# Half of the groups of three bias tables: the multiply by x goes from VectorE to ScalarE and GpSimd

## The chip, the core and the metric

The kernel runs on one core of a Trainium2 chip. The core has five engines that work side by side, each on its own queue of instructions in order: TensorE (PE in the profile) multiplies matrices into PSUM, VectorE (DVE) and ScalarE (ACT) compute element by element and reach both PSUM and SBUF, GpSimd (POOL) works on SBUF, and SyncE (SP) issues most of the transfers between the chip's main memory and SBUF. The metric is the device time of the whole program in microseconds; less is better. The time before is 1106.28 us, the median of three runs.

## What is computed

Attention over 4 batches, 8 heads, 576 positions and head size 64 with a bias that a small network makes from the positions, then two expert blocks, cut here to what matters:

```python
scores = (1 / sqrt(64)) * q @ k.T
rel = pos[:, None] - pos[None, :]
x = log1p(abs(rel)) / log1p(maximum(pos[:, None], 1))      # 576 x 576
h = maximum(x[..., None] * w1 + b1, 0)                     # 32 hidden units
bias = h @ w2                                              # one value per head
attn = softmax(scores + bias) @ v
y = moe1(attn)     # w_in, h * softmax(h), layer norm, w_out
out = moe2(y)      # sigmoid gate, value, w_out2
```

For one entry of the table, each hidden unit is either off or linear in x. So the bias of a head is a slope times x plus an offset, where slope and offset are sums over the units that are on at this x.

## The kernel before

**Bias tables.** The 576 rows of positions are made as five tables: tables 0 to 3 have 128 rows each, table 4 the last 64. `bias_tile(t)` makes table t group by group: `bias_mask` (lines 344 to 368) lets VectorE compare distances with thresholds, which gives a 0/1 mask of the units that are on (float16, 2048 elements in each partition), and `bias_grp` (lines 383 to 436) does the rest two groups later. Tables 0 to 3 have nine groups, table 4 has five.

**A group.** TensorE multiplies the masks with the weights into a PSUM bank (`bp`, line 409). For every pair of positions this gives 32 columns with the slope part (8 heads, 4 rows) and 32 with the offset part. For the later tables a group is done in two parts of 8 steps, each with a bank of its own from a pool of three (`ps_m`) that is shared with the transposes of q, k and of the attention's result. Then come two steps: the slope part times x into the tile `btmp` (a pool of two), and the sum with the offset part into the table (line 434, always VectorE). The first step has two forms, and the counter `nbg`, which goes up by one with every group over all tables, chooses:

```python
if nbg[0] % BD < (BD0 if t < 2 else BD1):          # 427
    dve.tensor_tensor(out=hg(tmp, 0), in0=hg(ps, 0), in1=xb_, op=ALU.mult)
else:
    act.activation(out=tmp, in_=ps[:, :, 0:32], func=ACTF.Copy)          # 430
    pool.tensor_tensor(out=hg(tmp, 0), in0=hg(tmp, 0), in1=xb_, op=ALU.mult)   # 431
```

BD is 4. For the first two tables BD0 = 0, so all groups take the second form: ScalarE copies the slope part out of PSUM (GpSimd does not read PSUM) and GpSimd multiplies. For tables 2, 3 and 4 BD1 = 4, so all groups take the first form.

**Where it stands in the program.** Tables 0 and 1 are made at the start and used from SBUF. Tables 4, 2, 3, in this order, are side work: `side_work` (line 955) hands out steps in turn, first alternating with the steps that decode and split the first expert's weights (`w1_steps`: ScalarE line 168, VectorE lines 169 to 173, GpSimd lines 177 and 639), then alone; five steps go with each tick of attention. A finished part of a table is stored to main memory by SyncE (lines 438 to 448) and loaded again when attention needs it. A tick is two heads of one block of rows: scores on TensorE (line 500), scores plus bias with the row maximum on VectorE (line 520), a factor (line 525) and the exponential on ScalarE (line 527), the float16 high part on ScalarE or VectorE (lines 538 and 536), the low part on GpSimd (lines 539 and 540), a transpose by DMA that SyncE issues (line 542), and the product with v on TensorE (line 560). There are 72 ticks. When tables and weights are ready, the first expert's steps take the place of the side work (lines 691 to 770); the second expert follows (lines 1025 to 1352).

**Order.** The program is written in this sequence, with a priority for attention's instructions; for most of it the order of each engine's queue is then laid out ahead of time with a simulated timeline, so a change of one instruction can shift the order of others. Once an engine runs, it takes its queue in order.

Of the kernel before, what the change touches and what calls it, by code (L numbers as in the profile page):

```python
# [51 lines left out]
TAILQ = 1  # L52
BD = 4
BD0 = 0
BD1 = 4
NFR = 12
SUMPRIO = 130
W2PRIO = 300
# [30 lines left out]
def attn_moe_kernel(  # L89
# [293 lines left out]
    def bias_grp(t, grp, bs):  # L383
# [18 lines left out]
        for big, a, n in parts:  # L402
# [21 lines left out]
            def hg(ap, o):  # L424
                return ap[:, :, o:o + 32].rearrange("p j (h g) -> p j h g", g=4)

            if nbg[0] % BD < (BD0 if t < 2 else BD1):
                dve.tensor_tensor(out=hg(tmp, 0), in0=hg(ps, 0), in1=xb_, op=ALU.mult)
# [992 lines left out]
```

## Time and profile before

| | us |
|---|---|
| median of three runs | 1106.28 |
| lowest, highest | 1100.22, 1108.24 |
| the profiled execution | 1103.77 |
| its span, first to last instruction | 1102.0 |

A profile shows one execution. Busy time is the time in which an engine ran an instruction; a wait is the idle time ahead of an instruction, put down to what released it. PE's granted clock is a share of full speed. Lines such as L428 are lines of the kernel; names left of the arrow are the tile that is written, right of it those that are read.

| whole span | busy us | share |
|---|---|---|
| TensorE matmuls | 911.8 | 83% |
| VectorE | 811.1 | 74% |
| ScalarE | 627.5 | 57% |
| GpSimd | 426.4 | 39% |

### The profile page before, as it was taken

The numbers are of one execution on the slowest core, as the hardware profiler recorded it, in microseconds if no ns is written. First come the engines' busy times: TensorE is split into PE (matmuls) and PEld (weight loads), VectorE is DVE, ScalarE is ACT, GpSimd is POOL, SyncE is SP. The second block draws the span as 40 slices with busy tenths as digits, with TensorE's granted clock in tenths as the row PEclk, the third lists the DMA queues.
The fourth block names the chain that finished last, engine by engine and source line by source line (L and its number), as shares of the span: only waits on it lengthen the run. The fifth ranks groups of instructions, "written<-read, shape, count | busy, mean of one in ns | idle before, by whom it ended". The sixth has DMA issues, their size and how long they took to land.

```text
span 1102.0 us, 24792 instructions
## 1 busy us (share of the span) xinstructions
PE 911.8 (83%) x9950; PEld 641.8 (58%) x9950; DVE 811.1 (74%) x1647; ACT 627.5 (57%) x1302; POOL 426.4 (39%) x365
## 2 busy tenths in 40 slices
PE   2554774678778889889999778798999899999998
PEld 2442553456456666767776456343477488488585
DVE  6797999897557776666774889989949568257453
ACT  4858567766567788877883667654323233123232
POOL 2566366473455466545552266749000000000000
PEclk9655666657898999999999899998999999999999
DMA  9948899698979899999957536621000100100000
GB/s 281 306 136 294 179 201 216 132 185 187 211 144 191 183 194 196 185 198 202 211 110 173 163 106 188 188 75 38 20 21 2 66 10 1 48 11 1 20 21 20
DMA packets 259715, 146.41 MB, mean 133 GB/s; under 512 B 216976, under 2 KB 229648, under 8 KB 259600
## 3 DMA queue, kind: packets, MB, share of 16 engines
q1 hardware_dynamic: 258064, 143.25, 55.1%
q0 software_dynamic: 1536, 1.58, 0.5%
q8 instruction: 78, 1.28, 0.5%
q14 instruction: 37, 0.30, 0.1%
HBM read 82.27 MB, written 20.05 MB: 93 GB/s over the span
## 4 chain that ended last, share of the span: by engine, by line
PE 29%; DVE 13%; issue 3%; ACT 2%; DMA 2%; POOL 1%; SPq 0%; POOLq 0%; DVEq 0%; ACTq 0%
PE prod L1229 14%; PE ops L1297 10%; DVE fr L1153 2%; DVE w2f L170 2%; DVE fs L1153 2%; DVE w2f L173 2%; PE x2ps L761 2%; DMA wraw<-in_moe_w_val_dram 1%; DVE gv L1135 1%; PE hps L702 1%; DMA wraw<-in_moe_w_gate_dram 1%; DVE w2f L169 1%; DVE w2s L1153 1%; PE xps L560 1%; DVE fr L1273 1%
## 5 line engine op out<-in xcount | busy, mean ns | idle before, releaser
L539 POOL TENSOR_TENSOR p<-p,p 128x1024 f16<-128x1024 f32 x72 | 154.5, 2146 | 154.3 <-ACT p L538 105.3
L1153 DVE TENSOR_TENSOR fr<-prod,fr 128x512 f32<-128x512 f32 (+1 forms) x154 | 91.8, 614 | 108.1 <-PE prod L1229 104.1
L1297 PE MATMUL ops<-w2f,gv 128*128 128x512 f16 x648 | 144.4, 382 | 4.3 <-DVE gv L1135 3.1
L527 ACT ACTIVATE p<-p,m,sc 128x576 f32<-128x576 f32 x144 | 124.0, 862 | 2.8
L761 PE MATMUL x2ps<-lt,w1f 128*128 128x128 f16 x1728 | 106.5, 221 | 12.7 <-DVE lt L750 11.9
L761 PEld LDWEIGHTS <-w1f 128*128 128x128 f16 x1728 | 100.7, 99 | 22.6 <-issue 18.8
L520 DVE CUSTOM_DVE_ANT_0 p<-s_ps,gk 128x576 f32<-128x576 f32 x144 | 104.2, 751 | 11.7 <-PE s_ps L500 8.6
L1297 PEld LDWEIGHTS <-gv 128*128 128x128 f16 x648 | 63.4, 98 | 79.6 <-DVE gv L1135 3.6
L1267 PE MATMUL s_ps<-xb,w2f 128*128 128x512 f16 x384 | 90.3, 392 | 18.0 <-DVE fr L1273 13.2
L409 PEld LDWEIGHTS <-mask 128*128 128x128 f16 (+1 forms) x1312 | 64.9, 122 | 65.8 <-issue 28.7
L500 PE MATMUL s_ps<-gk,qt 64*128 64x288 f16 (+1 forms) x960 | 94.8, 323 | 9.4 <-DVE m L520 5.4
L1229 PEld LDWEIGHTS <-w2f 128*128 128x128 f16 x1056 | 92.2, 98 | 11.7 <-issue 1.4
L560 PE MATMUL xps<-gk,pt 128*128 128x64 f16 (+1 forms) x2240 | 87.8, 202 | 12.1 <-DMA pt<-p 12.1
L560 PEld LDWEIGHTS <-pt 128*128 128x128 f16 (+1 forms) x2240 | 81.7, 107 | 25.2 <-DMA pt<-p 13.9
L702 PE MATMUL hps<-w1f,xt 128*128 128x512 f16 x312 | 77.9, 401 | 0.6 <-DVE qt L279 0.6
L409 PE MATMUL bp<-rhs,mask 128*128 128x64 f16 (+1 forms) x960 | 53.8, 227 | 29.2 <-DVE gb L434 14.8
L1267 PEld LDWEIGHTS <-w2f 128*128 128x128 f16 x384 | 38.2, 100 | 66.9 <-issue 26.0
L1134 ACT ACTIVATE gv<-fr 128x512 f16<-128x512 f32 (+1 forms) x60 | 34.7, 586 | 70.9 <-DVE fr L1287 65.7
L1229 PEld LDWEIGHTS <-w2s 128*128 128x128 f16 x792 | 69.2, 98 | 7.4 <-issue 0.3
L538 ACT ACTIVATE p<-p 128x1152 f16<-128x1152 f32 x54 | 62.6, 1159 | 14.1 <-DMA pt<-p 12.4
L525 ACT ACTIVATE m<-m,sc 128x1 f32<-128x1 f32 x144 | 40.5, 286 | 48.1 <-DVE m L520 48.0
L702 PEld LDWEIGHTS <-xt 128*128 128x128 f16 x384 | 37.2, 102 | 50.4 <-issue 16.4
(196 smaller groups left out, 1852.9 us busy)
## 6 DMA issues: line engine op xcount, KB each, us to landing
gk<-bias_d SPq DMA_DIRECT2D x24, 576.0 KB, 4.8
wraw<-in_moe_w_out_dram SPq DMA_DIRECT2D x20, 512.0 KB, 4.3
wraw<-in_moe_w_gate_dram SPq DMA_DIRECT2D x12, 512.0 KB, 4.1
wraw<-in_moe_w_val_dram SPq DMA_DIRECT2D x12, 512.0 KB, 3.8
sraw<-in_q_dram SPq DMA_DIRECT2D x12, 384.0 KB, 5.5
sraw<-in_k_dram SPq DMA_DIRECT2D x12, 384.0 KB, 3.8
sraw<-in_v_dram SPq DMA_DIRECT2D x12, 384.0 KB, 4.2
bias_d<-gk SPq DMA_DIRECT2D x8, 576.0 KB, 8.8
```

The lines of the kernel that those rows point to most:

```text
L409: pe.matmul(big[0:np_, jj // 8, o:o + 64], lhsT, rhs[i].rearrange("p c h g -> p (c h g)"), start=(i == 0), stop=(i == 1),)
L500: pe.matmul(ss[hh][p0:p1, n, 0:288], qt[rows, nr * ql + r, p0:p1], kt[rows, o:o + 288], start=(m == 0), stop=(m == 2))
L520: dve.tensor_tensor_reduce(out=pp[:, hh].rearrange("p (i j) -> p i j", i=2), in0=ss[hh][:, :, 0:288], in1=bi.rearrange("p (i j) -> p i j", ...
L527: act.activation(out=pp[:, hh], in_=pp[:, hh], func=ACTF.Exp, bias=m[:, 2 + hh:3 + hh], scale=col(C), accum_out=sm[:, c + hh:c + hh + 1])
L539: pool.tensor_tensor(out=p16[:, :, 640:1152], in0=pp[:, :, 0:512], in1=hi[:, :, 0:512], op=ALU.subtract)
L560: pe.matmul(o, a, b_, start=(n == 0), stop=(n == len(seq) - 1))
L702: pe.matmul(h, xt[:, xl, kk, off:off + 128], win16[:, 2 * kk + n, wl], start=(kk == 0 and xl == 0 and wl == 0), stop=(kk == 3 and xl == 1),)
L761: pe.matmul(ps[:, dc], wout16[:, f, wl, 128 * dc:128 * dc + 128], lt[:, ll, f], start=(n == 0), stop=(n == 23))
L1153: dve.tensor_tensor(out=out_, in0=a, in1=b, op=op)
L1229: pe.matmul(p[:, jf, 0:nn], w(wl, kk, jf), x(xl, kk), start=(m == 0), stop=(m == 5))
L1267: pe.matmul(ps[:, 0:n], w[:, 4 * (j // 4) + c, wl, o:o + 128], xx[:, 0:n, c, xl, :], start=(m == 0), stop=(m == 11))
L1297: pe.matmul(ps, gvs[j // 4][:, gl, j % 4, 128 * tt:128 * tt + 128], w2h16[2][:, j, wl], start=(m == 0), stop=(m == 35))
```

## The change

One constant:

```diff
-BD1 = 4
+BD1 = 2
```

For tables 4, 2 and 3 the test of line 427 now holds for groups with `nbg % 4` of 0 or 1 only. Groups with 2 or 3 take the second form: ScalarE's copy (line 430) and GpSimd's multiply (line 431) in place of VectorE's multiply (line 428). The sum of line 434 stays on VectorE and now takes GpSimd's result. Nothing else in the source differs; tables 0 and 1 are made as before.

## Rows read from the trace of the kernel before

**Rows 1.** Busy time of each engine by stage, whole core (columns in the first line)

```profile
core 0: us, PE busy (x) PEld busy (x) DVE busy (x) ACT busy (x) POOL busy (x), PEclk, DMA share, GB/s
110.00:270.00 160.00, 110.78 (x1517) 83.53 (x1518) 146.93 (x270) 101.80 (x213) 85.64 (x70) 0.63 0.88 183
270.00:600.00 330.00, 291.11 (x4248) 215.69 (x4249) 216.08 (x572) 246.49 (x546) 179.05 (x156) 0.96 0.92 181
...
800.00:1102.00 302.00, 292.75 (x2385) 212.16 (x2382) 174.16 (x313) 85.78 (x147) 0.00 (x0) 0.99 0.06 20
```

**Rows 2.** Waits, 110 to 270 us: us in total, times, longest

```profile
DVE btmp L428 <- PE bp L409: 3.2, 4, 1.4
...
DVE p L520 <- PE s_ps L500: 2.7, 3, 2.1
...
PE bp L409 <- DVE gb L434: 14.8, 9, 6.9
...
POOL p L539 <- ACT p L538: 18.5, 5, 6.0
...
SPq L542 <- POOL w1f L639: 24.1, 7, 6.0
```

**Rows 3.** Lines by form, 110 to 270 us: busy us, mean ns | idle before, releaser

```profile
L539 POOL TENSOR_TENSOR p<-p,p 128x1024 f16<-128x1024 f32 x17 | 36.5, 2145 | 30.8 <-ACT p L538 18.5 <-DVE sums L591 5.0 <-ACT sums L590 3.5
...
L358 DVE TENSOR_TENSOR mask<-dtab_sb,thr 128x2048 f16<-128x2048 f16 x18 | 27.5, 1527 | 0.0
...
L428 DVE TENSOR_TENSOR btmp<-bp,xs 128x256 f32<-128x256 f32 x44 | 24.4, 566 | 3.4 <-PE bp L409 3.2
...
L170 DVE SCALAR_TENSOR_TENSOR w1f<-wraw,w1f 128x512 int32<-128x512 int32 x10 | 10.9, 1093 | 0.0
...
L173 DVE SCALAR_TENSOR_TENSOR w1f<-wraw,w1f 128x512 int32<-128x512 int32 x6 | 6.7, 1120 | 0.1
...
L428 DVE TENSOR_TENSOR btmp<-bp,xs 64x256 f32<-64x256 f32 x2 | 0.8, 404 | 0.0
```

**Rows 4.** Timeline, VectorE and GpSimd near 172, VectorE near 234: start us, us

```profile
172.27 4.53 DVE L358 TENSOR_TENSOR mask<-dtab_sb,thr 128x2048 f16<-128x2048 f16 x1
...
172.08 2.14 POOL L539 TENSOR_TENSOR p<-p,p 128x1024 f16<-128x1024 f32 x1
...
174.55 1.15 POOL L639 TENSOR_TENSOR w1f<-wtmp,w1f 128x512 f16<-128x512 f32 x1
...
233.65 1.10 DVE L428 TENSOR_TENSOR btmp<-bp,xs 128x256 f32<-128x256 f32 x2
234.67 1.22 DVE L358 TENSOR_TENSOR mask<-dtab_sb,thr 128x2048 f16<-128x2048 f16 x1
```

**Rows 5.** Lines by form, 0 to 110 us, tables 0 and 1 (columns as Rows 3)

```profile
L430 ACT ACTIVATE btmp<-bp 128x256 f32<-128x256 f32 x14 | 5.2, 377 | 4.1 <-DVE gk L434 3.9 <-DVE acc L142 0.2
...
L431 POOL TENSOR_TENSOR btmp<-btmp,xs 128x256 f32<-128x256 f32 x14 | 16.1, 1153 | 9.7 <-ACT btmp L430 9.6
```

**Rows 6.** Instructions of single lines: count, ns min/median/max, first and last start us

```profile
L358 DVE TENSOR_TENSOR mask<-dtab_sb,thr x18: 1202/1222/4527, 126.5 to 250.9; 128x2048 f16<-128x2048 f16 x18
...
L170 DVE SCALAR_TENSOR_TENSOR w1f<-wraw,w1f x12: 671/683/2495, 95.3 to 199.6; 128x512 int32<-128x512 int32 x12
...
L173 DVE SCALAR_TENSOR_TENSOR w1f<-wraw,w1f x8: 679/800/2333, 96.6 to 200.4; 128x512 int32<-128x512 int32 x8
...
L428 DVE TENSOR_TENSOR btmp<-bp,xs x46: 403/580/599, 110.8 to 261.2; 128x256 f32<-128x256 f32 x44, 64x256 f32<-64x256 f32 x2
...
L431 POOL TENSOR_TENSOR btmp<-btmp,xs x25: 632/1524/2566, 21.9 to 82.6; 128x256 f32<-128x256 f32 x14, 128x512 f32<-128x512 f32 x11
...
L736 DVE TENSOR_SCALAR mm<-mm x18: 141/154/155, 295.8 to 663.3; 128x1 f32<-128x1 f32 x18
```

**Rows 7.** VectorE's waits over the whole span: us in total, times, longest

```profile
DVE mm L736 <- POOL mm L735: 11.0, 10, 1.8
...
DVE gk L434 <- POOL btmp L431: 5.1, 6, 2.0
```

## Prediction

> **What bounds the kernel now.** I read first the busy times by stage [rows 1]. The three later bias tables are built between 110 and 270 us. In that stage VectorE is busy 146.9 of 160 us (92%), TensorE 110.8, ScalarE 101.8, GpSimd 85.6, and the DMA engines stand at 0.88. After 270 us the picture turns: TensorE is busy 291 of 330 us and the DMA share is 0.92, and from 800 us on it is TensorE alone (293 of 302 us). So the change falls into the one stretch in which VectorE is the busiest engine, and what that stretch gains should move everything behind it as a block: attention blocks, expert blocks and the TensorE tail come in the order of the program, none of them starts by the clock.
>
> Second, the waits in that stage [rows 2]. VectorE's largest sum is 3.2 us (bias products that are late), and for attention's scores it waits 2.7; it lacks work only for moments, so an instruction less is time less, until another engine ends last. TensorE, in contrast, waits 14.8 us for the add of line 434 to give a PSUM bank back. GpSimd waits 18.5 us in five waits for ScalarE's cast of line 538, and the transposes of SyncE's queue wait 24.1 us for GpSimd's weight remainders (line 639). These three bear on the rivals.
>
> **The change part by part.** The group counter nbg stands at 18 when table 4 begins and runs 19 to 41 over the 5+9+9 groups of tables 4, 2 and 3. With BD1 = 4 all 23 groups, two parts each, take line 428: 46 multiplies, 44 of the large form and 2 of the small [rows 3]. With BD1 = 2 a group stays if nbg modulo 4 is 0 or 1. Those that leave are 19, 22, 23, 26, 27, 30, 31, 34, 35, 38 and 39: 11 groups, 22 parts, of which 2 (group 23) have 64 partitions.
>
> *Removed.* VectorE's instructions overlap a little, so I take the distance from start to start and not the duration: two multiplies start at 233.65 and the next instruction at 234.67, 0.51 us each [rows 4], where the group's mean is 0.566 [rows 3]. The small form has 0.404, scaled likewise 0.35. 20 x 0.51 + 2 x 0.35 = 10.9 us leave VectorE.
>
> *Added on ScalarE.* 22 copies from PSUM at 0.377 us [rows 5] are 8.3 us. ScalarE has 58 us idle in the stage, so I cost them at nothing. The cover has one hole: btmp has two buffers, so a copy can stand in ScalarE's queue until an add two parts back is done, with the exponentials of attention behind it. The next operand late would then be line 538's cast, and the transpose behind it. With full cost it is 8.3 us, which I count to the third rival.
>
> *Added on GpSimd.* 22 multiplies of the form that took 1.153 us on average in the first two tables [rows 5], 25.4 us; the shortest took 0.632 [rows 6], which would make 13.9. I take the mean, as VectorE will be as full as it was there. GpSimd goes from 85.6 to some 111 of 160 us. That is not full, but it isn't free: VectorE is held up while GpSimd runs. The row for it is the mask of line 358, 1.2 us at its shortest [rows 6] and 4.53 us at 172.27, while GpSimd ran line 539 from 172.08 and line 639 up to 175.70, with line 540 between [rows 4]. By groups, mean less shortest [rows 3, 6]: line 358 18 x 0.325 = 5.9 us, line 170 10 x 0.42 = 4.2, line 173 6 x 0.44 = 2.6; 12.7 us lost against 85.6 us of GpSimd, 0.148 us each. The 25.4 us added bring 25.4 x 0.148 = 3.8 us of new loss (with 13.9: 2.1). What is taken off VectorE does not suffer itself: line 428's longest is 0.599 [rows 6]. So lock-free work is traded for work that holds up others.
>
> [...]
>
> *Added wait.* The add of line 434 now waits for GpSimd instead of for VectorE's own multiply. Behind it in VectorE's queue stand masks, weight decoding and line 520 of attention, and ScalarE waits for that one. In the first two tables, all made this way, VectorE waited 5.1 us for 25 parts [rows 7], 0.204 each; 22 x 0.204 = 4.5 us. From below it is nothing. From above I take the other place where VectorE takes a result back from GpSimd, line 736: 11.0 us [rows 7] over 18 instructions [rows 6], 0.61 each, 13.4 us. I take 4.5, since it is the same operation, though GpSimd had less else to do there.
>
> *Unchanged.* Matmuls, masks, DMA issues and stores are the same in number. The last two groups (40, 41) stay on VectorE, so the hand-over of the last table gets no longer chain.
>
> *Sum.* -10.9 + 3.8 + 4.5 = -2.6 us. Against the profiled execution's own 1103.77 that is 1101.2; it lies 2.5 us below the median of the three runs, 1106.28, which would give 1103.7. I forecast 1103, nearer to the median because that is what is measured. Ends of this case: -10.9 + 2.1 + 0 = -8.8 (1097 from the median) and -10.9 + 3.8 + 13.4 = +6.3 (1112).
>
> **The rivals.**
>
> 1. *The relief goes through whole.* Neither stalls nor waits: 1106.3 - 10.9 = 1095. For it: VectorE's 92% and its small waits [rows 1, 2]. Against it: the mask's 4.53 us [rows 4], and that the chain now crosses three engines.
>
> 2. *Another bound takes over at once.* The DMA share is 0.88 in the stage and 0.92 after it [rows 1]; if the transposes set the pace, VectorE's free time turns into waits and nothing moves: about 1105. Against it: no wait of VectorE's for a DMA in the stage comes near the top, and SyncE's transposes wait for GpSimd rather than for the wire [rows 2].
>
> 3. *Slower: the multiply stands behind attention in GpSimd's queue.* GpSimd works in order. Five of the 17 large subtractions of line 539 in the stage [rows 3] waited 3.7 us each for ScalarE's cast [rows 2]. If the same share of the 22 multiplies, some 7, stands behind such a one, the add stands still on VectorE for that long, and everything behind it: 7 x 3.7 = 25.9. Then -10.9 + 3.8 + 25.9 = +18.8, about 1124 (1122.6 by the own time, 1125.1 by the median). It decides from a mean wait of (10.9 - 3.8)/22 = 0.32 us per part on; at 0.83 us the kernel is 1% slower. For it: first tables' GpSimd had no attention to serve, so 0.204 is measured under the easier condition; ScalarE's copies of this form waited there 3.9 us for adds, too [rows 5], and TensorE's 14.8 us for PSUM banks [rows 2] can only grow. Against it: the order of each queue is laid out with a simulated timeline, which puts the add where its operand is expected.
>
> 4. *Slower: each multiply stops VectorE for its full length*, as the mask of 4.53 us was stopped. 25.4 takes the place of 3.8: -10.9 + 25.4 + 4.5 = +19.0, about 1124 as well. Against it: 85.6 us of GpSimd now cost 12.7, not 85.6; most of VectorE's instructions read PSUM and run through.
>
> **How the numbers follow.** My forecast has 0.42, rival 1 0.16, rival 2 0.12, rival 3 0.24, rival 4 0.06. A difference of about 1% (11 us) is what a measurement of this kernel tells from no change. Even the whole relief of 10.9 us falls just short of that, so faster by over 1% holds only about half of rival 1 and a little of what a new order of the queues may bring: 0.13. Slower by over 1% is nearly all of rivals 3 and 4: 0.27. The rest, 0.60, lies within. The likeliest case's own range is 1097 to 1112; 8 in 10 takes in rival 1 below and reaches to rivals 3 and 4 above: 1094 to 1124.
>
> **What would show it.** Right: line 428 counts 24 and line 431 47; VectorE's busy time in the stage falls by 5 to 8 us; its wait for line 431 grows by about 4.5 us over the 22 parts, and masks keep a mean near 1.5 to 1.7 us. Wrong towards rival 1: that wait is near nothing and the last multiply of line 428, now at 261.2 [rows 6], comes some 11 us earlier. Towards rival 2: that multiply comes earlier, but the transposes or line 520 then wait, and the distance to the end grows. Towards rival 3: VectorE waits over 7 us for line 431 and the last multiply comes after 262. Towards rival 4: lines 358, 170 and 173 lose over 20 us to GpSimd. What I can't price is the new order that the whole program gets, since each queue is laid out anew; if the stage behaves as said and the end does not follow, that is the reason.

## The result, and the profile after

The changed kernel takes 1118.28 us (median of three runs, 1114.09 to 1120.82) where the kernel before took 1106.28. These two medians stand as 1.0108 to 1; the ratio recorded for the pair is 1.0127, 95% interval 1.0091 to 1.0162, and five later sets of 13 to 22 runs of the kernel before, with medians of 1102.82 to 1105.51, bear out the larger one. It is slower by 1.3%. The forecast was 1103 and no change that can be told; the time lies inside the range given, on the other side of no change.

The profiled execution of after took 1120.82 us with a span of 1119.0; that of before had a span of 1102.0. The profiles are thus 17.0 us apart and the medians 12.0, since the one profiled execution lies above its median and the other below. Three moments split the 17.0 us. The view of single lines gives them (count, ns min/median/max, start of the first and of the last instruction); here line 434 (the sum into the tables) and line 560 (the product with v) of the kernel before:

```profile
core 0 of [0], span 1102.0 us
...
L434 DVE TENSOR_TENSOR gb<-bp,btmp x46: 543/592/628, 111.4 to 261.8; 128x256 f32<-128x256 f32 x44, 64x256 f32<-64x256 f32 x2
...
L560 PE MATMUL xps<-gk,pt x2240: 192/193/262, 115.3 to 598.4; 128*128 128x64 f16 x150, 128*64 128x64 f16 x37
```

and of the changed kernel:

```profile
core 0 of [0], span 1119.0 us
...
L434 DVE TENSOR_TENSOR gb<-bp,btmp x46: 574/593/632, 117.1 to 272.4; 128x256 f32<-128x256 f32 x44, 64x256 f32<-64x256 f32 x2
...
L560 PE MATMUL xps<-gk,pt x2240: 192/193/261, 116.7 to 610.2; 128*128 128x64 f16 x150, 128*64 128x64 f16 x37
```

(In the fences "..." stands for lines left out; where no window is named, a line is from the whole span.) The last sum of the bias tables comes 10.6 us later (261.8 to 272.4), the last product of attention 11.8 us later (598.4 to 610.2), the end 17.0. So the stage of the change loses 10.6, attention behind it hands that on (+1.2), and the tail, from the last product to the end of the span, grows by another 5.2 (503.6 to 508.8), in a stretch where the change moved nothing. These three numbers, **last sum, last product, tail**, are given for every run below. How far they repeat is seen in two runs with the same order of work up to the end of attention, e9 for before and e10 for after: 261.0 and 596.8, 273.4 and 609.5. They hold to 1.6 us in these two. That is no bound, for single runs of the kernel before lie anywhere from 1099.0 to 1111.1 us, while the tails of kernels with one order behind attention agree within 2 us: most of the spread from run to run seems to lie ahead of the last product, and each profile below is one execution. Where it matters, the median is given beside it.

Busy times by stage, as [rows 1]:

```profile
core 0: us, PE busy (x) PEld busy (x) DVE busy (x) ACT busy (x) POOL busy (x), PEclk, DMA share, GB/s
...
110.00:270.00 160.00, 99.26 (x1347) 76.03 (x1347) 129.91 (x232) 103.49 (x230) 106.55 (x92) 0.61 0.86 178
270.00:600.00 330.00, 292.58 (x4229) 219.03 (x4230) 216.76 (x578) 248.27 (x550) 176.13 (x154) 0.94 0.91 181
```

VectorE is relieved (146.9 to 129.9) and GpSimd loaded (85.6 to 106.6), and both TensorE and VectorE do *less* in the same 160 us: the stage isn't short of engine time any more, it waits. The waits from 110 to 270 us, to set beside [rows 2] (us in total, times, longest):

```profile
PE bp L409 <- DVE gb L434: 21.1, 12, 3.9
POOL p L539 <- ACT p L538: 21.1, 7, 7.3
PE xps L560 <- DMA pt<-p: 20.8, 9, 4.6
...
ACT p L538 <- DMA pt<-p: 16.3, 7, 5.3
...
DVE gb L434 <- POOL btmp L431: 10.9, 7, 6.6
...
DVE xn L593 <- PE xps L560: 5.7, 1, 5.7
```

VectorE's longest kind of wait was 3.2 us in sum before; now it waits 10.9 us for the moved multiply, 6.6 of it in one place, and 5.7 for a product with v. The one long event, in the timeline (start, duration, engine, line; in brackets the idle time ahead and its releaser):

```profile
237.35 0.61 PE L560 MATMUL xps<-gk,pt 128*128 128x64 f16 x8 [4.03 <-DMA pt<-p]
237.39 1.16 ACT L538 ACTIVATE p<-p 128x1152 f16<-128x1152 f32 x1 [5.30 <-DMA pt<-p]
...
238.68 2.12 POOL L539 TENSOR_TENSOR p<-p,p 128x1024 f16<-128x1024 f32 x1 [7.35 <-ACT p L538]
238.98 0.64 ACT L430 ACTIVATE btmp<-bp 128x256 f32<-128x256 f32 x2
...
240.76 0.43 POOL L540 TENSOR_TENSOR p<-p,p 128x128 f16<-128x128 f32 x1
241.15 1.15 POOL L639 TENSOR_TENSOR w1f<-wtmp,w1f 128x512 f16<-128x512 f32 x1
242.26 1.66 POOL L431 TENSOR_TENSOR btmp<-btmp,xs 128x256 f32<-128x256 f32 x2
...
243.15 0.61 DVE L434 TENSOR_TENSOR gb<-bp,btmp 128x256 f32<-128x256 f32 x1 [6.62 <-POOL btmp L431]
...
243.81 0.42 PE L409 MATMUL bp<-rhs,mask 128*128 128x64 f16 x5 [3.93 <-DVE gb L434]
```

Read it from the top. A transpose lands late; the product on TensorE and the cast of line 538 on ScalarE wait for it. The copies of line 430 stand behind that cast, GpSimd's subtraction of line 539 waits 7.35 us for it, and the multiplies of line 431 stand behind the subtraction and a weight remainder. VectorE stands 6.62 us at the sum, and TensorE waits for the PSUM bank. Before, no such chain reached VectorE: its multiply read PSUM itself.

### The profile page after: what moved, and what is told of

It reads as the page before. It is cut to its first block, busy times and chain, and to the rows that moved or that the text cites. A ratio compares the mean times of both kernels' runs of the same rounds, so it can differ in the third digit from the quotient of the medians.

```text
span 1119.0 us, 24810 instructions
## 1 busy us (share of the span) xinstructions
PE 917.9 (82%) x9950; PEld 650.0 (58%) x9950; DVE 801.9 (72%) x1625; ACT 631.4 (56%) x1324; POOL 446.5 (40%) x387
## 4 chain that ended last, share of the span: by engine, by line
PE 31%; DVE 12%; DMA 3%; issue 2%; ACT 2%; POOL 1%; SPq 0%; ACTq 0%; POOLq 0%
PE prod L1229 13%; PE ops L1297 11%; DVE fs L1153 2%; DVE fr L1153 2%; PE x2ps L761 2%; PE s_ps L1267 2%; DVE w2f L170 2%; DMA wraw<-in_moe_w_val_dram 2%; DVE w2f L173 1%; DVE gv L1135 1%; PE hps L702 1%; DVE w2s L1153 1%; DMA wraw<-in_moe_w_gate_dram 1%; PE xps L560 1%; DVE w2f L169 1%
## 5 line engine op out<-in xcount | busy, mean ns | idle before, releaser
L761 PE MATMUL x2ps<-lt,w1f 128*128 128x128 f16 x1728 | 111.6, 226 | 13.8 <-DVE lt L750 10.9
L761 PEld LDWEIGHTS <-w1f 128*128 128x128 f16 x1728 | 105.1, 101 | 26.9 <-issue 19.6
L520 DVE CUSTOM_DVE_ANT_0 p<-s_ps,gk 128x576 f32<-128x576 f32 x144 | 104.1, 752 | 20.2 <-PE s_ps L500 16.6
L560 PE MATMUL xps<-gk,pt 128*128 128x64 f16 (+1 forms) x2240 | 91.2, 206 | 20.8 <-DMA pt<-p 20.8
L1267 PE MATMUL s_ps<-xb,w2f 128*128 128x512 f16 x384 | 92.1, 399 | 18.1 <-DVE fr L1273 14.2
L560 PEld LDWEIGHTS <-pt 128*128 128x128 f16 (+1 forms) x2240 | 85.6, 109 | 32.9 <-DMA pt<-p 23.6
L500 PE MATMUL s_ps<-gk,qt 64*128 64x288 f16 (+1 forms) x960 | 90.5, 320 | 10.1 <-DVE m L520 3.9
L702 PE MATMUL hps<-w1f,xt 128*128 128x512 f16 x312 | 75.6, 392 | 0.6 <-DVE qt L279 0.6
L431 POOL TENSOR_TENSOR btmp<-btmp,xs 128x256 f32<-128x256 f32 (+2 forms) x47 | 57.7, 1241 | 40.6 <-ACT btmp L430 39.8
```

What stands on the lines that cost most here:

```text
L500: pe.matmul(ss[hh][p0:p1, n, 0:288], qt[rows, nr * ql + r, p0:p1], kt[rows, o:o + 288], start=(m == 0), stop=(m == 2))
L520: dve.tensor_tensor_reduce(out=pp[:, hh].rearrange("p (i j) -> p i j", i=2), in0=ss[hh][:, :, 0:288], in1=bi.rearrange("p (i j) -> p i j", ...
L560: pe.matmul(o, a, b_, start=(n == 0), stop=(n == len(seq) - 1))
L702: pe.matmul(h, xt[:, xl, kk, off:off + 128], win16[:, 2 * kk + n, wl], start=(kk == 0 and xl == 0 and wl == 0), stop=(kk == 3 and xl == 1),)
L761: pe.matmul(ps[:, dc], wout16[:, f, wl, 128 * dc:128 * dc + 128], lt[:, ll, f], start=(n == 0), stop=(n == 23))
L1267: pe.matmul(ps[:, 0:n], w[:, 4 * (j // 4) + c, wl, o:o + 128], xx[:, 0:n, c, xl, :], start=(m == 0), stop=(m == 11))
```

## The experiments

"Order" below is the order of the instructions in each engine's queue. Each kernel's queues are laid out anew, so every edit moves it. Ratios are to the kernel before, run beside each experiment, with 95% intervals in brackets. Code is cut; "..." stands for what is left out.

### What the relief is worth, and what the load costs

**e1_relief.** The moved multiplies are left out altogether: the sums of the eleven groups take a tile of zeros.

```diff
+skip = t > 1 and nbg[0] % BD >= BD1
-tmp = bp_["tmp"].tile(...)[0:np_]
+tmp = (ztile if skip else bp_["tmp"].tile(...))[0:np_]
...
-if nbg[0] % BD < (BD0 if t < 2 else BD1):
+if skip:
+    pass
+elif nbg[0] % BD < (BD0 if t < 2 else BD1):
...
+pool.memset(ztile, 0.0)
```

> The relief by itself: in the 11 groups that the change moves, the multiply by x is left out altogether and the sum takes a tile of zeros, so the slope part of these groups is missing from the result; VectorE loses 22 multiplies and nothing is added to ScalarE or GpSimd, and no sum waits for another engine. If VectorE sets the pace of the stage, as the prediction's sum has it, the whole 10.9 us come through: 1106.3 - 10.9 = 1095, and the last sum of the tables ends near 251 us instead of 262. If the transposes by DMA set the pace (rival 2), the time stays within 3 us of the kernel before and VectorE's waits in the stage grow by what was taken off.

Ratio 0.9953 (0.9931 to 0.9974); last sum 255.8, last product 594.5, tail 504.4. Neither expectation holds: only 6.0 us reach the last sum and 3.9 the last product. From 110 us to the end of the last sum, the kernel before and e1 in this order, VectorE has less to do but stands idle for longer, 17.3 us where it was 10.2 (the length of the window less VectorE's busy time, the third in the row):

```profile
110.00:262.40 152.40, 103.18 (x1366) 77.24 (x1367) 142.21 (x259) 97.83 (x204) 85.64 (x70) 0.62 0.89 186
```

```profile
110.00:256.40 146.40, 97.68 (x1375) 74.55 (x1376) 129.13 (x238) 98.99 (x210) 85.10 (x69) 0.66 0.92 195
```

In the same windows TensorE's wait for transposes, ahead of the products with v, doubles (the edit moves line 560 to 563):

```profile
PE xps L560 <- DMA pt<-p: 12.1, 5, 6.3
```

```profile
PE xps L563 <- DMA pt<-p: 23.8, 11, 6.2
```

So a second bound stood close behind VectorE, and by these rows it lies in attention's own chain of cast, subtraction, transpose and product, at the transposes. How close is known no better than one layout tells: kernels further down that do the work of the kernel before, with a spare buffer, have 7.7 to 17.3 us of VectorE's idle time by this count.

**e5_nowait.** All work of the change is there, but the sums of the eleven groups take a tile of zeros, so that VectorE doesn't wait for GpSimd.

```diff
-a_part = hg(tmp, 0).rearrange(...)
+a_part = hg(ztile[0:np_] if t > 1 and nbg[0] % BD >= BD1 else tmp, 0).rearrange(...)
...
+pool.memset(ztile, 0.0)
```

> The change without its wait: the 11 groups are copied by ScalarE and multiplied by GpSimd as in the changed kernel and VectorE does not multiply, but the sum of these groups takes a tile of zeros, so no sum waits for GpSimd (the slope part of these groups is missing from the result). Against the first run (relief alone, 1099.9, last sum at 255.8 us) it has GpSimd's and ScalarE's work more, against the changed kernel (last sum at 272.4) only the wait less. If the wait of the sum is the loss (rival 3), the last sum comes within 4 us of 255.8 and the time is 1100 to 1104. If the load on GpSimd is the loss, through the transposes behind it or through VectorE's stalls, the last sum comes within 4 us of the changed kernel's, 268 to 276, and the time, without the 5 us after attention, is 1109 to 1114.

Ratio 1.0027 (1.0003 to 1.0052); last sum 263.8, last product 604.2, tail 504.3, between the two expectations. Against e1 the copies and multiplies cost 8.0 us at the last sum, with no sum waiting for them; against this run the wait costs the changed kernel a further 8.6. In these layouts the load by itself eats the relief. The moved multiplies do stand ahead of attention's transposes: of the 17 that SyncE issues from 110 us to the end of the last sum, 6 are released by one,

```profile
SPq L542 <- POOL btmp L431: 19.5, 6, 4.3
```

but in sum the transposes wait for GpSimd hardly longer than before (35.6 us before, 37.5 here, 40.0 in the changed kernel, each to the end of its last sum).

**e3_both_extra** and **e2_pool_extra.** The kernel before with the copies and multiplies added on scratch tiles (e3), or the multiplies alone (e2); nothing is relieved and nobody reads the product.

```diff
+if t > 1 and nbg[0] % 4 >= 2:
+    act.activation(out=scr[0][0:np_], in_=ps[:, :, 0:32], func=ACTF.Copy)     # not in e2
+    pool.tensor_tensor(out=hg(scr[1][0:np_], 0), in0=hg(scr[0][0:np_], 0), in1=xb_, op=ALU.mult)
```

> All of the change's new work, none of its relief and none of its wait: VectorE multiplies in all groups, and in the 11 groups ScalarE also copies the slope part to a scratch tile and GpSimd multiplies that into another one. Nobody reads the result. If the wait of the sum is the loss (rival 3), this costs 2 to 6 us over the kernel before (stalls, and PSUM banks held until ScalarE's copy is done): 1108 to 1112, less than the changed kernel's 12 although VectorE has 10.9 us more to do. If the work itself is the loss, it costs the changed kernel's 12 us plus the relief that is missing here: 1125 or more. The queues after attention stand in the same order as in the kernel before, so the stretch from the last product with v (598.4 us before) to the end should take 504 us as before, and not 509 as in the changed kernel.

> GpSimd's load by itself: the kernel before, VectorE still multiplies in all groups, and beside it GpSimd does 22 multiplies of the same form on a scratch tile that nobody waits for. By the prediction's stall term (0.148 us of VectorE per us of GpSimd, 14 to 25 us added) it costs 2 to 4 us: about 1109. If each multiply stops VectorE for its full length (rival 4), it costs 19 to 25 us: 1125 to 1131. If the loss of the change is only the wait of the sum (rival 3), this kernel lies within 4 us of the kernel before, and the place behind late casts in GpSimd's queue costs VectorE nothing, since no sum of VectorE's waits for it; a few transposes are issued later.

e3: ratio 1.0154 (1.0110 to 1.0199), last sum 280.2, last product 617.7, tail 504.4. e2: 1.0163 (1.0134 to 1.0192), 282.1, 618.0, 502.7. Both lose some 18 to 20 us at the last sum, and both times (1122.27 and 1123.35) fall short of the 1125 that their dearer theories asked for. e2 is a poor control: with nothing to tie them, its multiplies were placed in clusters from 54.7 us on, other places than the change's. Together they say that 22 multiplies on GpSimd that nobody waits for can cost about 20 us where VectorE has not been relieved.

**e11_act_extra.** The copies alone.

```diff
+if t > 1 and nbg[0] % 4 >= 2:
+    act.activation(out=scr[1][0:np_], in_=ps[:, :, 0:32], func=ACTF.Copy)
```

> The kernel before, with the 22 ScalarE copies of line 430 added on a scratch tile that nobody reads: nothing removed, no GpSimd work, no add that waits. Theory that the load which costs is GpSimd's (its multiplies stand ahead of the weight remainders and of the subtraction for the transposes): the copies cost little, last add of line 434 within 3 us of 261.8 and the last product with v within 4 us of 598.4. Rival, that ScalarE's copies delay the casts of line 538 and the exponentials: both come 8 us or more late, as with copies and multiplies together (18.4 and 19.3 us).

```profile
L428 ACT ACTIVATE scr<-bp x22: 360/366/385, 110.7 to 253.7; 128x256 f32<-128x256 f32 x20, 64x256 f32<-64x256 f32 x2
```

The 22 copies run in the places of the change (110.7 to 253.7) and cost the stage nothing in the profiled execution: last sum 259.9, last product 598.5, tail 504.0. That execution lies 2.7 us below the median of its ten runs, though, and the ratio, 1.0042 (1.0018 to 1.0066), puts 2 to 7 us on this kernel, copies and new layout together. Beside the 1.5% of e3 most of the load's cost is GpSimd's; that the copies are free isn't shown.

### Is it the wait of the sum?

**e12_tmp4.** The changed kernel with four buffers for the products.

```diff
-tmp=enter(st, "tmp", 2)
+tmp=enter(st, "tmp", 4)
```

> The changed kernel with four buffers for the products in place of two, so that a copy on ScalarE need not wait for the add two parts back, and GpSimd can run further ahead. If the wait of the add comes from too few buffers: VectorE's wait for line 431 falls from 10.9 us under 4, and the last product with v comes 5 us or more before 610.2. If it comes from GpSimd's order (the multiply stands behind the subtraction of line 539, which waits for ScalarE's cast): the wait stays over 7 us, and the last product with v stays within 3 us of 610.2.

Half of each theory came true: the wait (from 110 to 280 us) falls under 4 us,

```profile
DVE gb L434 <- POOL btmp L431: 3.4, 4, 1.3
```

as too few buffers would have it, and yet the last sum stays at 272.4 and the last product at 609.0 (tail 503.8; ratio 1.0102, 1.0083 to 1.0122). VectorE's idle time fell by 9.2 us against the changed kernel, but its losses (its instructions taking longer than their shortest; counted further down) rose by 7.2, and 2.0 us more of other work stood ahead of the last sum. The named wait is where the lateness showed, not its size.

**e4_shift** moves the groups with counter 0 and 1 modulo 4 in place of 2 and 3 (twelve groups); **e8_prio** puts copy and multiply of the moved groups ahead of other work in the layout.

```diff
-if nbg[0] % BD < (BD0 if t < 2 else BD1):
+if t > 1 and nbg[0] % BD >= BD1:
```

```diff
+with tc.high_priority(PRIO if t > 1 else 0):
     act.activation(out=tmp, in_=ps[:, :, 0:32], func=ACTF.Copy)
     pool.tensor_tensor(out=hg(tmp, 0), in0=hg(tmp, 0), in1=xb_, op=ALU.mult)
```

> The same change with the other groups: those with counter modulo 4 of 0 and 1 go to ScalarE and GpSimd, 12 groups, and those with 2 and 3 stay on VectorE. The queues after attention stand as in the kernel before. If the changed kernel's loss is one of the way it is done (sums behind late casts), the last sum ends 5 to 15 us later than before here too, at 267 to 277, the waits of line 434 for GpSimd are 5 us or more, and the time is 1110 to 1120, without the 5 us that the changed kernel loses after attention. If it hung on where exactly these 11 groups stand, the last sum ends before 262 and the time is at or under 1106.

> The changed kernel with ScalarE's copy and GpSimd's multiply of the moved groups laid out at attention's priority, so that they stand ahead of casts and subtractions that come later. If the multiply's place in the queues is the cause (rival 3), the waits for line 431 fall from 10.9 us to under 4 and the last sum comes at 262 to 267; without the 5 us after attention that makes 1103 to 1109. If the work on GpSimd is the cause wherever it stands, the last sum stays within 3 us of 272 and the time is 1111 to 1116, since what the sums gain the transposes lose.

e4: ratio 1.0053 (1.0036 to 1.0070), last sum 267.4, last product 605.4, tail 504.0, wait for line 431 1.9 us. e8: 1.0044 (1.0024 to 1.0064), 266.2, 602.7, 503.3, wait 5.8. Both lose less than the change, with waits of either size, and neither reaches the kernel before. e4's last sum is where the theory had it and its wait is not; in e8 the last sum came into the range for the multiply's place in the queue, but the wait did not fall under 4 us.

### The tail: an order that nobody asked for

Behind the end of attention the source is the same in both kernels, but the queues' order there is not: on all five engines it differs. **e9_man_before** and **e10_man_after** give both kernels one order from there on, that of the source, by hand.

```diff
+ctx.enter_context(tc.manual_schedule(engines={...}))          # all five
 w2_p = enter(ctx, "w2", 1, "right")
...
-with tc.issue_after(seen.ins):
+with nullcontext():
...
-with tc.issue_after(glob["so"].ins):
+with nullcontext():
```

> The kernel before, but from the end of attention on every queue keeps the order of the source, not the order that the scheduler lays out. This is the base for the next run. Up to the last product with v nothing changes: it should come within 1 us of 598.4. The distance from there to the end will be some other than 503.6, as the order is another; its size is not what the run is for.

> The changed kernel with the same fixed order behind attention as the run before, so that the two have one late order. Theory that 5.2 of the 17.0 us come from the new order which the scheduler gave to the queues behind attention: the distance from the last product with v to the end is then the same in the two runs within 1.5 us, and their whole difference is the 11.8 us that the last product with v is late. Rival, that the 5.2 us come from what the stage leaves behind (late weights, buffers, transfers), whatever the order: the distance is then again about 5 us longer in this run, and the whole difference 17.

```profile
core 0 of [0], span 1362.7 us
...
L560 PE MATMUL xps<-gk,pt x2240: 189/193/261, 116.1 to 596.8; 128*128 128x64 f16 x150, 128*64 128x64 f16 x37
```

```profile
core 0 of [0], span 1376.2 us
...
L560 PE MATMUL xps<-gk,pt x2240: 190/193/261, 116.0 to 609.5; 128*128 128x64 f16 x150, 128*64 128x64 f16 x37
```

The source's order costs 262 us (ratios 1.2371 and 1.2453), but the two tails are 765.9 (e9, first fence) and 766.7 (e10): 0.8 apart, not 5.2. (e9's last product was expected within 1 us of 598.4 and came 1.6 us ahead. The spans are 13.5 us apart, the medians 8.4, as e10's profiled execution lies 4.9 us above its median.) **e16_xs3_after** asks from the other side: the changed kernel with a third buffer for the tables of x, which keeps after's order behind attention.

```diff
-NXS = 2
+NXS = 3
```

> The changed kernel with three buffers for the tables of x in place of two. Nearly the same layout of the stage as the changed kernel, and behind attention its order, not that of the kernel before. If the late order is the cause of the last 5.2 us, the distance from the last product with v to the end is 508.8 within 1.5 us here too; if it is the luck of one execution, it is nearer to 503.6.

Its tail is 1123.4 - 613.4 = 510.0 (ratio 1.0177, 1.0144 to 1.0209; last sum 278.2). The loss sits early in the tail, at the last products of the first expert (line 761): before, after and e16, in this order, end them at

```profile
L761 PE MATMUL x2ps<-lt,w1f x1728: 216/219/314, 306.8 to 687.1; 128*128 128x128 f16 x192
```

```profile
L761 PE MATMUL x2ps<-lt,w1f x1728: 216/219/314, 314.0 to 706.1; 128*128 128x128 f16 x192
```

```profile
L761 PE MATMUL x2ps<-lt,w1f x1728: 216/219/315, 319.4 to 708.7; 128*128 128x128 f16 x192
```

which is 88.7, 95.9 and 95.3 us behind their last products. Where the order behind attention is that of before, whatever happened ahead of it (e2 to e6, e8, e12 to e14, e17), and in e1, e7 and e11, which differ from it in few places, the tail is 502.7 to 504.4, with the stage of the changed kernel ahead of it too (e14). That the order makes the 5.2 us is shown.

### Is it the move, or the layout it got?

**e7_p16_before** is the kernel before with one more buffer for attention's float16 weights, no work added, and **e6_p16_after** the changed kernel with the same:

```diff
-NP160 = 2
+NP160 = 3
```

> The kernel before with the same third buffer. It shows how much of the previous run's gain has to do with the change. If the two buffers only hurt once sums wait behind the casts, this kernel stays within 3 us of the kernel before (1101 to 1107). If late transposes hold up attention in the stage anyway, it gains 3 to 8 us (1096 to 1101), and then it beats both kernels.

> The changed kernel with three buffers instead of two for attention's float16 pair from the start, so that a cast need not wait for a transpose of two ticks before. In the changed kernel the cast of line 538 waited 16 us for transposes in the stage, GpSimd waited 21 us for that cast, and the longest wait of a sum (6.6 us) stood behind it. If that chain is the cause, the longest wait for line 431 falls under 2 us, their sum under 4, and the last sum comes 6 to 10 us earlier than 272.4; the time is 1103 to 1109. If the transposes are late for another reason, the stage ends within 3 us of 272 and the time is 1111 to 1116.

e7: ratio 1.0041 (1.0019 to 1.0063), last sum 269.7, last product 607.0, tail 503.8. e6: 1.0069 (1.0039 to 1.0099), 271.1, 605.5, 503.9. In e6 the sums' wait in the stage falls to 2.6 us, as asked of it if the chain of casts were the cause, but the last sum comes only 1.3 us earlier. e7 did neither of what was expected: it lost. In the profiles a spare buffer costs the kernel before 8.6 us at the last product (4.4 in the medians, e7's profiled execution lying 2.7 above its own), and on top of it the change costs nothing there. So the stage's 11.8 us could be the luck of one layout. Three more pairs were made to tell, before and after with the same disturbance: three buffers for the products (**e13**, **e14**), four (**e15**, and e12 from above), four masks (**e17**, **e18**).

```diff
-tmp=enter(st, "tmp", 2)
+tmp=enter(st, "tmp", 3)
```

```diff
-NMASK = 3
+NMASK = 4
```

> The kernel before with three buffers for the products in place of two: no work is added or taken, but the queues up to the end of attention are laid out anew; behind attention they stand as before. It is one half of a pair with the next run, and shows how far a new layout by itself moves the stage. If the layout weighs little: last sum of line 434 within 2 us of 261.8 and last product with v within 2 us of 598.4. If it weighs as much as the change: 5 us or more from them, to either side. Distance from there to the end 503.6 within 1.5 us, as the late order is the same.

> The changed kernel with three buffers for the products; its queues behind attention stand as in the kernel before. Theory that the move of the products costs the stage time of its own: last product with v some 6 to 12 us behind that of the run before. Rival that the 11.8 us of the stage are for the most part the luck of one layout: less than 3 us behind, or ahead. In both cases the distance from there to the end is 503.6 within 1.5 us; with 508.8 the late order would not be the cause of the last 5.2 us.

> The kernel before with four buffers for the products, the pair of the changed kernel with four (last sum 272.4, last product with v 609.0, end 1112.8). Theory that the move costs the stage time of its own: last product with v at 597 to 603. Rival, that the layout does it: at 606 or later. Behind attention this kernel has a third order, which neither of the two has, so its distance to the end is open; it is a further price of an order.

> The kernel before with four buffers for masks in place of three, the first half of a third pair: no work added, the same order behind attention as before. If a new layout weighs little: last product with v within 2 us of 598.4; distance from there to the end 503.6 within 1.5 us.

> The changed kernel with four buffers for masks. Theory that the move costs the stage time of its own: last product with v some 4 to 12 us behind that of the run before. Rival, luck of a layout: less than 3 us behind, or ahead. Behind attention it has the third order, that of the kernel before with four buffers for the products: the distances to the end should be alike within 1.5 us in the two.

| pair, before / after | ratio to before | last sum | last product | tail |
|---|---|---|---|---|
| as they stand | 1 / 1.0127 | 261.8 / 272.4 | 598.4 / 610.2 | 503.6 / 508.8 |
| e13 / e14, 3 product buffers | 1.0071 / 1.0090 | 266.7 / 269.2 | 606.1 / 605.4 | 504.2 / 504.0 |
| e15 / e12, 4 product buffers | 1.0022 / 1.0102 | 262.4 / 272.4 | 598.8 / 609.0 | 506.5 / 503.8 |
| e17 / e18, 4 masks | 1.0001 / 1.0079 | 261.3 / 270.2 | 596.6 / 607.7 | 504.1 / 504.9 |
| e7 / e6, attention's buffer | 1.0041 / 1.0069 | 269.7 / 271.1 | 607.0 / 605.5 | 503.8 / 503.9 |

(e15 and e18 share a third order behind attention; their tails, 506.5 and 504.9, are 1.6 apart, a little more than the 1.5 expected. The 95% intervals: e13 1.0043 to 1.0099, e14 1.0060 to 1.0121, e15 1.0004 to 1.0040, e17 0.9977 to 1.0025, e18 1.0052 to 1.0107.)

By their expectations e13 (+7.7 at the last product) and e14 (0.7 ahead of it) speak for the layout, e15, e17 and e18 for the move; both are at work. The change costs 10.6, 2.5, 10.0, 8.9 and 1.4 us at the last sum: 6.7 in the mean, and by the spread of the five a 95% interval of 1.2 to 12.1. In the ratios the mean is 0.66% (0.12 to 1.21), about 7 us. At the last product it is 6.2 with an interval of -2.1 to 14.5, which does not exclude nothing; nor do the ratios of the four new pairs alone, 0.51% (0.0 to 1.0), without the first, which holds the 5.2 us of the tail and is itself to be explained. All five pairs have one sign at the last sum and in the ratios. So the move is in all likelihood slower by itself, by an amount that five pairs hardly fix, and the rest of the 1.3% is layout: in the kernels before alone, the last product lies anywhere from 596.6 to 607.0, and as it stood the kernel had one of the good ones. No kernel in this study that does the whole computation is faster than the kernel before.

The same pairs give the terms of the prediction's sum. From 110 us to the end of the last sum VectorE's time is split into idle time; losses, which are mean less shortest of lines 169, 170, 173, 251, 358, 366, 536 and 659, times their count (the same shortest for all kernels); and the rest, its work (changes in us):

| pair | work | losses | idle | of it wait for L431 | sum |
|---|---|---|---|---|---|
| as they stand | -8.9 | -0.7 | +20.2 | 10.9 | +10.6 |
| 3 product buffers | -10.0 | +7.1 | +5.4 | 5.9 | +2.5 |
| 4 product buffers | -9.7 | +6.2 | +13.5 | 3.4 | +10.0 |
| 4 masks | -8.9 | +1.4 | +16.5 | 6.4 | +8.9 |
| attention's buffer | -10.1 | +6.4 | +5.1 | 2.6 | +1.4 |
| mean | -9.5 | +4.1 | +12.1 | 5.8 | +6.7 |
| predicted | -10.9 | +3.8 | +4.5 | 4.5 | -2.6 |

By the same split, good to a few tenths, the steps from the kernel before over e1 and e5 to the changed kernel are these, each between two single layouts:

| step | work | losses | idle | sum |
|---|---|---|---|---|
| before to e1: the relief | -10.0 | -3.1 | +7.1 | -6.0 |
| e1 to e5: the load | +0.3 | +5.8 | +1.8 | +8.0 |
| e5 to after: the wait | +0.6 | -3.3 | +11.3 | +8.6 |

## Why the prediction was wrong, step by step

The groups that the steps below use, after the change, 110 to 270 us (beside [rows 3, 5]):

```profile
L358 DVE TENSOR_TENSOR mask<-dtab_sb,thr 128x2048 f16<-128x2048 f16 x18 | 30.5, 1695 | 1.4 <-PE bp L409 1.4
...
L431 POOL TENSOR_TENSOR btmp<-btmp,xs 128x256 f32<-128x256 f32 x20 | 20.8, 1053 | 0.7 <-DVE m L520 0.6
...
L170 DVE SCALAR_TENSOR_TENSOR w1f<-wraw,w1f 128x512 int32<-128x512 int32 x10 | 9.1, 911 | 0.0
...
L430 ACT ACTIVATE btmp<-bp 128x256 f32<-128x256 f32 x20 | 7.3, 371 | 4.4 <-PE bp L409 2.2 <-DVE gb L434 2.0
L173 DVE SCALAR_TENSOR_TENSOR w1f<-wraw,w1f 128x512 int32<-128x512 int32 x6 | 7.1, 1189 | 0.0
```

**Removed, -10.9: right within 1.4 us.** Line 428 runs 24 times, line 431 47 times, as counted. VectorE's work fell by 8.9 here and by 9.5 in the mean of the pairs. The sign asked for in the prediction, busy time down by 5 to 8 us in the stage, was badly put: it fell by 17.0 between 110 and 270 us, because with the delay some of the work slid out of that window.

**Copies at nothing: not contradicted, and not shown.** 22 copies at 0.37 us; in e11's profile the stage doesn't feel them, in its ten runs the kernel is 0.42% slower. The hole in the cover that was named (a copy that waits for the sum two parts back) is 2.0 us in the row of line 430.

**GpSimd's multiplies, 25.4: right in size.** The large form took 1.053 us (predicted 1.153), GpSimd stands at 106.6 of 160 us (predicted 111).

**Losses of VectorE beside GpSimd, +3.8: right in the mean, at +4.1**, though anywhere from -0.7 to +7.1 in the single pair, so the fit is in part luck. The masks' mean of 1.695 is inside the 1.5 to 1.7 given. Rival 4 is out: lines 358, 170 and 173 lose 18 x 0.488 + 10 x 0.236 + 6 x 0.503 = 14.2 us, against 12.7 before and the 20 it asked for. The Trainium skill (SBUF — State Buffer, Who interferes with whom) says of a VectorE instruction with two SBUF inputs and a GpSimd instruction that reads SBUF that they contend, and that the one of the two that issues second is blocked for the whole of the other; the single masks of up to 3.1 us here don't speak against it, but 21 us more of GpSimd brought far less than 21 us of blocking.

**Wait for the product, +4.5: too small here, about right in the mean.** 10.9 us in seven waits where 22 x 0.204 was put; 5.8 over the pairs. The price from the first two tables was taken under the easier condition, as rival 3 said, and rival 3's mechanism is the event at 243.15. Its signs came, a wait over 7 us and the last multiply after 262 (271.9), but its size didn't: it asked for 25.9.

**The step that failed: "an instruction less is time less".** That sentence was taken from VectorE's 92% and its small waits, and rival 2 was put aside because "no wait of VectorE's for a DMA in the stage comes near the top". A table of waits shows the bound that ends last now. It can't show how close the next one is, because VectorE, being late itself, hid it. e1 shows what became of the relief in one layout: with nothing added anywhere, VectorE's work falls by 10.0 us and its idle time grows by 7.1, so that 6.0 come through to the last sum and 3.9 to the last product. Over the pairs the sum lacked the same thing, the idle time which is not the named wait: 20.2 - 10.9 = 9.3 us here and 12.1 - 5.8 = 6.3 in the mean (95% interval 0.1 to 12.5). Of the 6.3, 2.7 are VectorE's wait at line 593 for a product with v (5.7 us here, 1.6 before), which stands behind attention's transposes; the rest is spread over many lines. This is rival 2's mechanism in part, VectorE's free time turned into waits behind transposes, though a transpose itself takes no longer: from issue to landing 6.9 us in the median before, 7.1 in e1 and 6.8 after the change.

What the load does is less clear. GpSimd also makes the low parts of attention's weights and the remainders of the expert's weights, so the change puts its work onto that second chain, and e5's row has transposes released by the moved multiplies. But of e5's 8.0 us, 5.8 are VectorE's losses, the very term that was priced, here at 0.29 us for each us of GpSimd in place of 0.148, and only 1.8 are idle time; of the 20.3 us between e11 and e3, whose difference is GpSimd's multiplies with VectorE not relieved, 10.7 are losses and 8.3 idle time. So a price of what stands behind the multiplies in GpSimd's own queue isn't shown.

**What was named and not priced: the new order.** "If the stage behaves as said and the end does not follow, that is the reason." The stage did not behave as said, but the end got 5.2 us worse on top for this reason, shown by e9, e10 and e16. Inside the stage the layouts scatter by as much as the whole effect.

In all, of the 17.0 us between the profiles 5.2 are the order behind attention. Of the 11.8 ahead of it 6.2 may be put down as the move's own mean price at the last product, with the wide interval given above, and 5.6 as what the layout of the stage and the two executions add here; in e9 and e10, which have the orders of the two kernels up to there and nearly equal tails, the medians are 8.4 apart, so some 3 us may be the executions'. That the time lies inside the range is luck: the upper end was set by rivals 3 and 4, whose 25.9 and 25.4 us did not come. Why the one late order is slower than the other wasn't tried.

## What to carry to other kernels

Before work is taken off the busiest engine, ask how far behind it the next bound is, and whether the work goes onto that one: leaving the work out altogether is one run, and it gives the ceiling of any such change (here 0.5%), to within the luck of a layout. An engine with idle time is not free (GpSimd's 22 multiplies that no sum waited for cost 8 to 20 us at the last sum); price what its instructions hold up on other engines and what stands behind them in its queue, not only who reads their result. Where queues are laid out anew with every edit, disturb both kernels in the same harmless way a few times before a difference of 1% is put down to the edit.

## What the runs showed of the hardware

VectorE's losses beside GpSimd don't follow GpSimd's busy time: with 85.6 us of it they were 20.1, with 106.6 us 19.4, and in e11, with 86.5 us, 13.7. Which instructions meet seems to count for more than how many; a rate per us, as the prediction used, held only in the mean of five pairs. Nor are they only the instructions with two tiles of SBUF as inputs: line 536, a cast that reads one, took 0.747 us at its shortest and 1.71 in the kernel before when it started while GpSimd ran line 639:

```profile
218.06 2.13 POOL L639 TENSOR_TENSOR w1f<-wtmp,w1f 128x512 f16<-128x512 f32 x1
...
219.10 1.71 DVE L536 CAST p<-p 128x1152 f16<-128x1152 f32 x1
```
